# One attention decode step on one core: the first load, wq, issued as two DMAs of 16 and 112 rows instead of one of 128

## The chip, the core and the metric

The kernel runs on one core of a Trainium2 chip. The metric is the device time of one execution in microseconds (us); runs of the kernel before lie between 2516.09 and 2516.40 us, with a median of 2516.12 us. The core has a matrix engine (PE, whose weight loads are listed as PEld), a vector engine (DVE), a scalar engine (ACT), GpSimd (POOL) and a synchronisation engine (SP). In this kernel SP issues nearly all loads from device memory (HBM) into on-chip memory (SBUF, 128 partitions); sixteen DMA engines carry them out. "SPq" in the profile is SP's time spent on issuing.

## What is computed

One query token passes through an attention block with a long cache, and through a small gated feed-forward block. The two results are mixed with a gate made from the same token. There are 32 heads of 128 elements, and each head has 65536 cached keys and values.

```python
g = sigmoid((x * gate_w).sum(-1, keepdims=True))        # x: [1, 1, 512]
q = (x @ wq).reshape(1, 1, 32, 128).transpose(0, 2, 1, 3)   # wq: [512, 4096]
scores = einsum("bhqd,bhkd->bhqk", q, k_cache) * 128 ** -0.5
p = softmax(scores)
o = einsum("bhqk,bhkd->bhqd", p, v_cache)
a = o.transpose(0, 2, 1, 3).reshape(1, 1, 4096) @ wo
b = (silu(x @ w_gate) * (x @ w_up)) @ w_down
out = g * a + (1 - g) * b
```

The two caches have 32 x 65536 x 128 bf16 elements each, 537 MB each; wq is 4.19 MB. The profile counts 1087.64 MB read from HBM in one execution.

## The kernel before

**Streaming.** A head's keys are read in pairs of tiles of 8.39 MB: each of the 128 partitions receives one run of 65,536 bytes. `K_bufs` holds two such pairs and `V_buf` one. For each K tile DVE multiplies the keys by the query (L283) and adds halves of the products (L295, L313); PE adds up what is left (L517), DVE folds it into scores (L324), ACT takes exponentials (L421), and PE multiplies the values by them (L541). There are 64 pairs. The first two and the last two are written out by hand; `prologue` holds the first two, and loops run over the rest.

**Order.** There is no scheduler: each engine runs its instructions in the order in which the code emits them, and `wait` (L171) puts a wait on a semaphore ahead of one. An `Events` object (L28) counts: each DMA adds 16 to its semaphore when it has landed. SP's order decides the order of the loads. A K or V load is issued when its buffer is free, that is, when the instruction that used the buffer last has counted (`load_v` L202, `load_k` L211).

**The start.** `prologue` (L566) begins with two small loads on ACT's queue: the token x into `xT` and the gate weights into `gwT`, 128 rows of 8 bytes each. On SP's queue come, without any wait between them, wq into the first half of `V_buf` (L570), the two tiles of the first K pair (L189), the second K pair (L185), and w_gate and w_up (L576). Row p of the wq load goes into partition p and is one run of 32 KB (four rows of the matrix, 4 x 4096 x 2 bytes). SP then waits until PE has finished with wq (L628) and issues w_down into its place (L629).

**What uses wq.** PE waits for x and for wq (L585, L586) and forms the queries in eight groups of four heads (`query_row`, L590, matmuls at L593). Every matmul reads all 128 partitions of wq, so none can begin before the last row has landed. The query of head 0 is spread over the partitions as `q_sb` (L622). DVE's first product (L283, called at L634) waits for this and for the first K tile.

**What follows in SP's queue.** The third K pair is issued when PE has finished with the first (L669, `pe_D` at 2), the first V pair when the feed-forward block has finished with `V_buf` (L698), and the fourth K pair when PE has finished with the second (L709). From there on the loops run.

Of the kernel before, what the change touches and what calls it, by code (L numbers as in the profile page):

```python
# [10 lines left out]
P = 128  # L11
# [29 lines left out]
def kernel(  # L41
# [18 lines left out]
    _, H, Sk, Dh = A_k_cache.shape  # L60
    D = A_x.shape[2]
    F = B_w_gate.shape[1]
    KT = D // P
# [21 lines left out]
    V_buf = ring.tile([P, PAIR * Dh], bf16, name="V_buf")  # L85
# [51 lines left out]
    def v_view(n):  # L137
        return {N - 4: K_half[0][1], N - 3: V_half[0], N - 2: V_half[1], N - 1: K_half[1][1]}[n]

    sync, act, dve, pool, pe = nc.sync, nc.scalar, nc.vector, nc.gpsimd, nc.tensor  # L140
# [13 lines left out]
    x_in, gw_in, wq_in, ka_in, kb_in, kc_in, wg_in, wu_in, wd_in, vA_in, vB_in = (  # L154
        Events(nc, n, 16)
        for n in ("x_in", "gw_in", "wq_in", "ka_in", "kb_in", "kc_in", "wg_in", "wu_in", "wd_in", "vA_in", "vB_in")
    )
# [13 lines left out]
    def wait(engine, events, value):  # L171
        key = id(engine), id(events)
        value -= taken.get(key, 0)
        if seen.get(key, 0) < value:
            engine.wait_ge(events.sem, value)
            seen[key] = value
# [34 lines left out]
    def load_k(m):  # L211
        if m in (0, M - 1):
            for n in range(2):
                load_tile(K_half[m % 2][n], A_k_cache, 2 * m + n, (k_in[1] if m else ka_in, kb_in)[n])
        else:
            load_pair(K_bufs[m % 2], A_k_cache, m, k_in[m % 2] if m > 1 else kc_in)
# [349 lines left out]
    def prologue():  # L566
        with nc.allow_non_contiguous_dma(reason="small"):
            x_in(act.dma_start(out=xT, in_=A_x[0, 0, :].rearrange("(p t) -> p t", t=KT)))
            gw_in(act.dma_start(out=gwT, in_=gate_w.rearrange("(p t) -> p t", t=KT)))
        wq_in(sync.dma_start(  # L570
            out=V_buf[:, : KT * H * Dh], in_=A_wq.rearrange("(p t) f -> p (t f)", t=KT)
        ))
        load_k(0)
        load_k(1)
        for w, (rows, events) in enumerate(((B_w_gate, wg_in), (B_w_up, wu_in))):
# [7 lines left out]
        dv(dve.memset(rs, 0.0))  # L583

        wait(pe, x_in, 16)  # L585
        wait(pe, wq_in, 16)  # L586

        wait(pe, dv, marks["ones_b"])

# [34 lines left out]
        for c in range(3, H // QUAD):  # L624
# [28 lines left out]
            out=rest[0:1, :], in0=gval[0:1, :], scalar1=-1.0, scalar2=1.0, op0=ALU.mult, op1=ALU.add  # L653
# [40 lines left out]
        for i, a in enumerate(a_ps):  # L694
            pe.matmul(
                a, lhsT=ones_f[0:1, 0:1], rhs=b_sb[:, i * HD : (i + 1) * HD], start=True, stop=False
# [102 lines left out]
    with tc.tile_critical(sync_engine=mybir.EngineType.Pool):  # L799
        prologue()  # L800
        for m in range(2, M):
            if m < M - 1:
                sync_step(m)
            tell_of_v(m - 2)
        sync_end()
        sync_out()
        with act.Fori(0, GROUPED, QUAD) as first:
            scalar_round(first)
        scalar_end()
        with dve.Fori(0, (M - 4) // (2 * MH)):  # L810
            vector_round()
        vector_end()
        with pe.Fori(0, (M - 4) // 2):
            for m in range(2):
                tensor_step(m)
        tensor_end()
        for engine in (pe, act, dve):
            engine.sem_inc(done.sem, 1)

        pool.wait_ge(done.sem, 4)  # L820
        pool.sem_clear(range(first_sem.num, last_sem.num + 1))
        sync.wait_ge(out_in.sem, 16)
        sync.sem_inc(out_in.sem, -16)
# [30 lines left out]
```

## Time and profile before

| what | value |
|---|---|
| median of three runs | 2516.12 us |
| the profiled execution, its own time | 2516.13 us |
| its span, first to last instruction | 2514.3 us |
| DVE busy | 2003.3 us, 80% |
| PE busy | 1489.5 us, 59% |
| ACT busy | 186.9 us, 7% |
| read from HBM | 1087.64 MB |
| mean rate over the span | 433 GB/s |
| wq: issue to landing | 12.4 us, one DMA of 4096 KB |
| x: issue to landing | 12.6 us, 1 KB |
| first K pair, two tiles: issue to landing | 21.9 and 31.2 us, 4096 KB each |
| second K pair: issue to landing | 50.0 us |

"Issue to landing" runs from the start of the issuing instruction to the semaphore count that tells that all data are there. The sixteen DMA engines work through what is queued, so for all but the first load it contains the time spent behind earlier loads. Busy time of an engine is the sum of its instructions' times; an engine that is not the bottleneck may idle without cost. In the page, the span is cut into 40 equal slices of 62.86 us; the line "DMA" gives the busy share of the DMA engines in tenths and "GB/s" the rate in each slice.

### The profile page before, as it was taken

What the parts mean: (1) busy time and instruction counts of PE and PEld (TensorE: products, weight loads), DVE (VectorE), ACT (ScalarE), POOL (GpSimd) and SP (SyncE); (2) the same over time, 40 slices, a digit from 0 to 9 for tenths busy, and PEclk for the clock granted to TensorE, in tenths of its full rate; (3) what the DMA queues carried; (4) which work ended last, traced back from release to release, by engine and by line L of the source; (5) the groups of instructions that cost most, each with busy time, mean ns of one, the idle gap of its engine ahead of it and who ended that gap; (6) DMA issues with size and microseconds to landing.
All of it is one profiled execution on the core that took longest, in us unless ns stands there. A gap on an engine that the chain in (4) does not pass through costs nothing. (4 is left out here: it accounts for less than half of the span.)

```text
span 2514.3 us, 15594 instructions
## 1 busy us (share of the span) xinstructions
PE 1489.5 (59%) x6525; PEld 615.9 (24%) x6525; DVE 2003.3 (80%) x678; ACT 186.9 (7%) x512; POOL 0.7 (0%) x6
## 2 busy tenths in 40 slices
PE   3655746656557456465575564655755646557569
PEld 1322222222222222222222222222212222222223
DVE  6897887877878878779788788787787877977881
ACT  1000000000000000000000000000000000000000
POOL 0000000000000000000000000000000000000000
PEclk8777878778778787787787777877877778778789
DMA  9999999999999999999999999999999999999999
GB/s 413 440 434 433 435 435 435 434 435 434 434 434 434 434 434 434 434 434 436 434 435 436 435 435 434 435 435 434 435 434 434 434 434 435 435 434 434 435 428 394
DMA packets 22606, 1087.80 MB, mean 433 GB/s; under 512 B 2753, under 2 KB 3266, under 8 KB 4546
## 3 DMA queue, kind: packets, MB, share of 16 engines
q1 hardware_dynamic: 22306, 1087.65, 99.9%
q8 instruction: 7, 0.11, 0.0%
q10 hardware_dynamic: 288, 0.00, 0.0%
q14 instruction: 5, 0.04, 0.0%
HBM read 1087.64 MB, written 0.00 MB: 433 GB/s over the span
## 5 line engine op out<-in xcount | busy, mean ns | idle before, releaser
L283 DVE TENSOR_TENSOR K_buf<-K_buf,q_sb 128x16384 bf16<-128x16384 bf16 (+1 forms) x129 | 1112.0, 8620 | 348.2 <-DMA K_buf<-in_A_k_cache_dram 348.2
L517 PE MATMUL S_ps<-K_buf,ident_b 128*128 128x512 bf16 (+1 forms) x1104 | 383.8, 522 | 861.0 <-PEq L513 834.8
L541 PE MATMUL O_ps<-V_buf,P_sb 128*4 128x512 bf16 x3968 | 866.8, 379 | 30.2 <-PEq L513 29.8
L541 PEld LDWEIGHTS O_ps<-V_buf,P_sb 128*4 128x4 bf16 x3968 | 333.0, 85 | 561.8 <-issue 59.3
L295 DVE TENSOR_TENSOR K_buf<-K_buf 128x4096 bf16<-128x4096 bf16 (+1 forms) x127 | 433.7, 3415 | 3.1
L517 PEld LDWEIGHTS S_ps<-K_buf,ident_b 128*128 128x128 bf16 x1104 | 132.9, 125 | 1090.1 <-issue 1030.2
L313 DVE TENSOR_TENSOR K_buf<-K_buf 128x8192 bf16<-128x8192 bf16 x60 | 265.5, 4425 | 2.0
L396 ACT ACTIVATE O_sb<-O_ps 4x512 f32<-4x512 f32 x63 | 63.3, 1005 | 1705.1 <-PE qm_ps L531 1675.1
L324 DVE TENSOR_REDUCE S_sb<-S_ps 128x128 f32<-128x512 f32 x128 | 88.1, 689 | 105.4 <-PE S_ps L517 103.3
L534 PE MATMUL qm_ps<-diag,ones_f 128*128 128x128 f32 x126 | 33.7, 354 | 72.2 <-PEq L513 70.2
L549 PE MATMUL oh_ps<-ident_f,O_sb 4*128 4x1 f32 x504 | 64.3, 244 | 19.6 <-PEq L513 19.6
L549 PEld LDWEIGHTS oh_ps<-ident_f,O_sb 4*128 4x128 f32 x504 | 60.7, 186 | 49.7 <-issue 49.7
L295 DVE TENSOR_TENSOR T_sb<-K_buf 128x2048 bf16<-128x2048 bf16 x60 | 72.8, 1214 | 0.0
L517 PE MATMUL S_ps<-T_sb,ident_b 128*128 128x512 bf16 x240 | 64.7, 391 | 0.0
L534 PEld LDWEIGHTS qm_ps<-diag,ones_f 128*128 128x128 f32 x126 | 21.7, 216 | 76.3 <-issue 76.3
L396 ACT ACTIVATE bias<-top 128x1 f32<-128x1 f32 x32 | 6.5, 203 | 436.7 <-DVE top L334 436.7
L537 PE MATMUL tot_ps<-rs,ones_f 128*128 128x2 f32 (+1 forms) x126 | 24.7, 266 | 17.8 <-PEq L513 17.7
L396 ACT ACTIVATE oT<-whole_o,rg 32x1 f32 (+1 forms) x115 | 33.8, 294 | 4.6
L421 ACT ACTIVATE P_sb<-S_sb,bias 128x256 bf16<-128x256 f32 x62 | 31.5, 508 | 1.0
L537 PEld LDWEIGHTS tot_ps<-rs,ones_f 128*128 128x128 f32 x126 | 20.2, 202 | 36.8 <-issue 36.8
L517 PEld LDWEIGHTS S_ps<-T_sb,ident_b 128*128 128x128 bf16 x240 | 20.7, 96 | 15.9
L330 DVE TENSOR_REDUCE m<-S_sb 128x1 f32<-128x512 f32 x32 | 22.0, 686 | 1.1
(68 smaller groups left out, 209.8 us busy)
## 6 DMA issues: line engine op xcount, KB each, us to landing
K_buf<-in_A_k_cache_dram SPq DMA_DIRECT2D x4, 4096.0 KB, 32.5
V_buf<-in_A_v_cache_dram SPq DMA_DIRECT2D x2, 4096.0 KB, 21.4
V_buf<-in_A_v_cache_dram SPq DMA_DIRECT2D x4, 2048.0 KB, 18.2
V_buf<-in_A_wq_dram SPq DMA_DIRECT2D x1, 4096.0 KB, 12.4
K_buf<-in_A_v_cache_dram SPq DMA_DIRECT2D x1, 4096.0 KB, 30.2
K_buf<-in_A_wo_dram SPq DMA_DIRECT2D x7, 512.0 KB, 16.2
K_buf<-in_A_v_cache_dram SPq DMA_DIRECT2D x3, 1024.0 KB, 23.2
V_buf<-in_B_w_gate_dram SPq DMA_DIRECT2D x1, 1792.0 KB, 54.5
```

Source lines behind the costliest of these rows:

```text
L283: return own[0](dve.tensor_tensor(out=K, in0=K, in1=q_rep, op=ALU.mult))
L295: ins = dve.tensor_tensor(out=to, in0=K[:, :, 0:half], in1=K[:, :, half : 2 * half], op=ALU.add)
L313: dve.tensor_tensor(out=K[:, :, 0:half], in0=K[:, :, 0:half], in1=K[:, :, half:], op=ALU.add).then_inc(c_S[0], 1)
L324: return own[0](dve.tensor_reduce(out=S_sb[h % 2][:, g * NB : (g + 1) * NB], in_=S_ps[n % 2], axis=AXIS.X, op=ALU.add))
L330: (dv_max if h else dv_first)(dve.tensor_reduce(out=m_sb[:, 0:1], in_=S_sb[h % 2], axis=AXIS.X, op=ALU.max))
L396: return act.activation(out=out, in_=in_, func=ACT.Copy, scale=scale)
L421: return act.activation(out=out, in_=S_sb[h % 2][:, b * PAIR : b * PAIR + count], func=ACT.Exp, bias=bias[:, 0:1], scale=scale, accum_out= ...
L517: ins = pe.matmul(S_ps[n % 2][:, start:stop, :], lhsT=ident_b, rhs=src[:, start:stop, c : c + QUAD], start=(c == 0), stop=(c == width - QUAD),
L534: pe.matmul(mT, lhsT=ones_f, rhs=diag, start=True, stop=True).then_inc(pe_m.sem, n)
L537: pe_t(pe.matmul(tot[:, :n], lhsT=ones_f, rhs=rs[:, :n], start=True, stop=True))
L541: ins = pe.matmul(O_ps, lhsT=probs[:, j : j + 4], rhs=view[:, j : j + 4, :], start=(opens and j == start), stop=(closes and j == stop - 4),)
L549: ins = pe.matmul(oh, lhsT=O_sb[:, c * Dh : (c + 1) * Dh], rhs=ident_f[0:4, c : c + 1], start=(opens and c == 0), stop=(c == 3),)
```

## The change

The load of wq is issued as two DMAs on the same queue, the first with rows 0 to 15, the second with rows 16 to 127. Source, destination, bytes and the length of a row are the same. The wait of PE asks for a count of 32 instead of 16, as two DMAs now add 16 each.

```diff
-        wq_in(sync.dma_start(
-            out=V_buf[:, : KT * H * Dh], in_=A_wq.rearrange("(p t) f -> p (t f)", t=KT)
-        ))
+
+        for a, b in ((0, 16), (16, P)):
+            wq_in(sync.dma_start(
+                out=V_buf[a:b, : KT * H * Dh], in_=A_wq.rearrange("(p t) f -> p (t f)", t=KT)[a:b]
+            ))
         load_k(0)
         load_k(1)
...
         wait(pe, x_in, 16)
-        wait(pe, wq_in, 16)
+        wait(pe, wq_in, 32)
```

On SP the instruction list becomes one DMA longer: a copy of 16 x 16384 elements and one of 112 x 16384 stand where one of 128 x 16384 stood. The other engines keep their lists.

## The prediction

> **What bounds the kernel now.** I began with the page's slices, to see whether the load stream ever pauses.
>
> ```profile
> span 2514.3 us, 15594 instructions
> ...
> DMA  9999999999999999999999999999999999999999
> GB/s 413 440 434 433 435 435 435 434 435 434 434 434 434 434 434 434 434 434 436 434 435 436 435 435 434 435 435 434 435 434 434 434 434 435 435 434 434 435 428 394
> ```
>
> Between the third slice and the 38th the rate stays at 433 to 436 GB/s, although DVE and PE work unevenly. Only the first slice and the last two fall below. The stream sets the time: 1087.65 MB at 434.5 GB/s take 2503 us of the 2514.3, and the rest is start and end. DVE, busy 80%, follows the loads:
>
> ```profile
> DVE K_buf L283 <- DMA K_buf<-in_A_k_cache_dram: 348.2, 64, 21.9
> ```
>
> That is from the list of waits (total us, times, longest): DVE waits for 64 loads of keys, 348.2 us in all. So DMA time lost anywhere is paid at the end, and DMA time gained early is earned. Next the timeline of the start (start us, duration, engine, line):
>
> ```profile
> 0.89 0.40 SPq L570 DMA_DIRECT2D V_buf<-in_A_wq_dram  x1
> 0.90 0.41 ACTq L568 DMA_DIRECT2D xT<-in_A_x_dram  x1
> ...
> 1.35 0.89 SPq L189 DMA_DIRECT2D K_buf<-in_A_k_cache_dram  x2
> ...
> 2.28 0.61 SPq L185 DMA_DIRECT2D K_buf<-in_A_k_cache_dram  x1
> ...
> 13.52 3.47 PE L593 MATMUL S_ps<-V_buf,xT 128*1 128x512 bf16 x8 [13.52 <-DMA xT<-in_A_x_dram]
> ...
> 18.66 0.25 ACT L396 ACTIVATE q_sb<-qm_ps 128x128 bf16<-128x128 f32 x1
> ...
> 23.26 8.69 DVE L283 TENSOR_TENSOR K_buf<-K_buf,q_sb 128x16384 bf16<-128x16384 bf16 x1 [21.90 <-DMA K_buf<-in_A_k_cache_dram]
> ```
>
> SP issues its first loads with no gap. x, only 1 KB, lands as late as wq, so PE starts at 13.52. The first query is ready at 18.91, yet DVE starts at 23.26, when the first K tile lands: the query has 4.35 us to spare, the load stream nothing. Last, the DMA rates of the first 4 us, in slices of 0.1 us (packets counted where they start):
>
> ```profile
> GB/s 0 0 0 0 0 0 0 0 0 0 0 0 0 0 0 0 0 0 0 2294 983 655 0 328 0 655 328 0 0 0 0 0 0 0 0 0 0 328 983 1311
> ```
>
> The first row starts at 1.9 us, 1.0 after the issue of wq. Sixteen rows (each 32 KB adds 328 to a slice) start up to 2.7 us, one on each DMA engine; the next ones start from 3.7.
>
> **The unit.** At 434.5 GB/s the sixteen engines carry 27.2 GB/s each, so a row of 32 KB takes 1.21 us. The 128 rows are eight to an engine, 9.7 us; wq's 12.4 us from issue to landing are 1.0 before the first row, these 9.7, and 1.7 of slow start and completion.
>
> **The change, part by part.** (1) *One more issue on SP.* The rows beside it take 0.40 (wq), 0.45 (half of 0.89) and 0.61 us. All issues behind the first move back by 0.4 to 0.6 us, the last, w_up, from 3.53 to about 4.0. The cover is wq itself: its rows keep the engines busy until about 12.4 us, and the K tile behind it needs only to be queued by then. Without that cover it would cost those 0.4 to 0.6. Should a full queue hold SP back longer, w_up is what waits; its data are used at 61.8 us, and SP's next own work is at 25.02. Cost 0.
>
> (2) *The wait for 32.* No instruction is added on PE, and what stands behind this wait (all queries, then the first product) is released by x anyway, which lands with the last wq rows. Cost 0; a count that comes up to 4.35 us later than now, relative to the K tile, is still hidden.
>
> (3) *The start.* With one row for each engine the first DMA could be set up faster. The issue takes 0.40 us now and the engines' first rows start over some 0.7 us, so at most 1.1 us are to be had; at worst nothing. I take 0.2: most of the 1.0 us between issue and first data is neither of the two.
>
> (4) *Where the rows go.* Every load in this trace that matters fills all 128 partitions, each engine serving its own eight. The flat 434.5 GB/s shows sixteen paths of 27.2, but not whether a path belongs to the engine that reads or to the eight partitions that are written. If to the engine: one row, then seven, eight as before, 0 us. If to the partitions, and to eight neighbours: the 16 rows go through two paths, eight in series, 9.7 us in place of 1.21, a loss of 8.5 us during which fourteen paths idle. The other 112 rows then have 14 paths with eight rows each, 9.7 against 8.5, and 1.2 more are lost if nothing overlaps. So 0 to +9.7, with no row nearer to one end than to the other: no load here writes a part of the partitions. I take the end at the partitions without the last 1.2, +8.5. I choose it because a DMA of 16 rows is the first thing here that sends all sixteen engines into one eighth of the memory, and nothing in the trace frees that from sharing.
>
> [...] No run before this one shows a load on fewer partitions.
>
> *Sum.* 2514.3 + 0 + 0 - 0.2 + 8.5 = 2522.6 us of span; the profiled execution had 1.8 outside it (2516.13), so 2524.4. Its time and the median (2516.12) are the same. Nothing gives the 8.5 back: the K tiles, the third K pair (issued at 55.90, on PE's word) and every later load move along. With SP's V loads landing 24.4 us after issue and needing 19.3 for 8.39 MB, about 5 us of work stays queued ahead of each, so an engine that is late by 8.5 sets the pace, and others that are less late only use up that reserve.
>
> **The rivals.**
>
> *A. Not slower: the path belongs to the engine.* Then only (3) is left: 2516.1 - 0.2 = 2515.9, at the very best 2515.0. [...] Against it: only loads over all partitions have been seen. It decides from the point where the 16 rows land within about 4 us of their issue (1.0 + 1.21 + the 1.7).
>
> *B. A small loss.* Four engines to a path in the 16 rows, four row-times in place of one, 3 x 1.21 = 3.6 us, and the 112 rows dealt out evenly: 2516.1 + 3.6 - 0.2 = 2519.5, say 2519 to 2521. For it: 16 rows are few. Against it: 112 rows in sevens do not fit groups of eight.
>
> *C. A large loss.* The 112 rows are dealt to the engines in turn, so that sixteen neighbours are always written at once. With four to a path, 32 row-times in place of 8: 24 x 1.21 = 29 us, 2545; with eight, 56 x 1.21 = 68 us, 2584. For it: the trace does not show which rows an engine takes. Against it: in the 128-row loads the same dealing would have shown as a rate far below 434.5.
>
> *D. The code does not do what it says.* Both DMAs stand on SP in the order written, so I give this nothing of its own.
>
> **How the numbers follow.** The forecast, sharing in the 16 rows and in the sevens, has 0.46 (its own range 2520.5 to 2529); A 0.25; B 0.13; C 0.08; 0.08 is left for what I have not thought of, 0.03 of it faster by more than A, 0.05 slower. The range from 2515.0 to 2529 takes in A, B and nearly all of the forecast, and leaves out C and most of the rest. For this kernel a change of less than 0.2%, 5.0 us, counts as none: the bounds are 2511.1 and 2521.2. Slower is nearly all of the forecast (0.44), C, 0.05 of the rest and a bit of B: 0.59. The same is A, most of B and the low end of the forecast: 0.38. Faster, beyond anything that (3) can give: 0.03.
>
> **What would show it.** The 16-row DMA's landing: 7 (four to a path: 1.0 + 4.85 + 1.7) to 12 us after its issue if the partitions set the rate, about 4 if the engines do. The 112-row DMA's landing: near 21 us after the first issue in place of 12.4. PE's first matmul near 22 us, DVE's first product near 31.8, the third K pair's issue near 64. The first slice falls from 413 GB/s by up to 8.5 x 434.5 / 62.86 = 59, less if only some engines are late by that much; the slices behind it keep 434. Wrong would be a first slice at 413 with the same start of DVE's product at 23.3 (A), or a loss that appears in later slices, for which I have no mechanism.

## The result and the profile after

The changed kernel takes 2525.74 us (median of 7 runs, 2524.84 to 2526.16), the kernel before 2516.14 (7 runs, 2516.08 to 2516.89): 9.6 us more, a ratio of 1.0037 with a 95% interval of 1.0025 to 1.0048. The profiled execution took 2526.16 us, with a span of 2524.3.

The page of the changed kernel, its span, its DMA share and its rate in 40 slices:

```profile
span 2524.3 us, 15595 instructions
...
DMA  9999999999999999999999999999999999999999
GB/s 354 444 426 435 433 435 434 432 433 435 433 435 435 436 433 433 432 434 434 437 435 435 432 433 433 433 436 436 436 433 433 432 433 434 438 434 435 433 430 387
```

The first slice falls from 413 to 354 GB/s. Over its 62.86 us these 59 GB/s are 3.7 MB, the work of 8.5 us at 434.5 GB/s. Behind it little is added: in the next stretch of 62.86 us the rate is 434 in place of 440 GB/s, another 0.9 us, and from there to 2388.6 us it is 434 in both. So the loss is made at the start and kept. The busy share, nine tenths and more everywhere, does not show it: an engine that carries a row slowly counts as busy (a share of 1.02 at 243 GB/s, below).

The timeline of the start, and the answers on the two wq loads (KB each, us from issue to landing):

```profile
0.89 0.85 SPq L572 DMA_DIRECT2D V_buf<-in_A_wq_dram  x2
...
1.79 0.90 SPq L189 DMA_DIRECT2D K_buf<-in_A_k_cache_dram  x2
...
22.90 3.57 PE L595 MATMUL S_ps<-V_buf,xT 128*1 128x512 bf16 x8 [22.90 <-DMA V_buf<-in_A_wq_dram]
```

```profile
V_buf<-in_A_wq_dram SPq DMA_DIRECT2D x1, 3584.0 KB, 21.5
...
V_buf<-in_A_wq_dram SPq DMA_DIRECT2D x1, 512.0 KB, 6.5
```

```profile
32.48 8.69 DVE L283 TENSOR_TENSOR K_buf<-K_buf,q_sb 128x16384 bf16<-128x16384 bf16 x1 [31.12 <-DMA K_buf<-in_A_k_cache_dram]
```

The issue of the second DMA costs SP 0.45 us. The 112 rows land about 22.8 us into the span (13.3 before), PE starts at 22.90 (13.52), now released by wq and no longer by x, and DVE begins at 32.48 (23.26), still released by the K tile. DVE is 9.2 us late. Near the end PE is 9.3 us late, in the kernel before and then in the changed one:

```profile
2384.54 13.97 PE O_ps L541 x64
```

```profile
2393.84 13.97 PE O_ps L541 x64
```

The span grows by 10.0: the other 0.7 of this execution arise at the end, where the last load of wo lands at 2519.82 in place of 2509.81.

The rate while the 112 rows are written, and below it that of the kernel before at full stream (from and to in us, length, busy time of PE, PEld, DVE, ACT and POOL, PE's clock, DMA share, GB/s; a packet counts where it starts):

```profile
5.30:20.40 15.10, 0.00 (x0) 0.00 (x0) 0.00 (x0) 0.00 (x0) 0.00 (x0) 1.00 1.02 243
```

```profile
13.50:23.20 9.70, 9.65 (x54) 3.24 (x55) 0.00 (x0) 4.36 (x10) 0.00 (x0) 1.00 1.01 433
```

How long one row takes can be read from the DMA queue's own lines: packets that started in a stretch, their MB, and their time as a share of what sixteen engines have in it. The kernel before from 1 to 3 us comes first, then the changed kernel from 1 to 3 and from 7 to 20.2 us:

```profile
q1 hardware_dynamic: 16, 0.52, 94.2%
```

```profile
q1 hardware_dynamic: 16, 0.52, 180.2%
...
q1 hardware_dynamic: 96, 3.15, 92.7%
```

The first sixteen rows took 1.88 us each before (94.2% of 2 us) and 3.60 in the changed kernel, and 96 of the 112 rows took 2.04, where a row at full stream takes 1.21. At 243 GB/s the 3.67 MB of the 112 rows take 15.1 us, not 8.4: most of the loss lies in the larger DMA.

### The profile page after: what moved, and what is told of

The parts are those of the page before. It is cut to its first block, busy times and chain, and to the rows that moved or that the text cites. A ratio compares the mean times of both kernels' runs of the same rounds, so it can differ in the third digit from the quotient of the medians.

```text
span 2524.3 us, 15595 instructions
## 1 busy us (share of the span) xinstructions
PE 1489.2 (59%) x6525; PEld 615.5 (24%) x6525; DVE 2003.4 (79%) x678; ACT 186.9 (7%) x512; POOL 0.7 (0%) x6
## 5 line engine op out<-in xcount | busy, mean ns | idle before, releaser
L534 PEld LDWEIGHTS qm_ps<-diag,ones_f 128*128 128x128 f32 x126 | 21.9, 218 | 76.5 <-issue 76.5
L595 PE MATMUL S_ps<-V_buf,xT 128*1 128x512 bf16 x32 | 10.6, 470 | 22.9 <-DMA V_buf<-in_A_wq_dram 22.9
## 6 DMA issues: line engine op xcount, KB each, us to landing
V_buf<-in_A_wq_dram SPq DMA_DIRECT2D x1, 3584.0 KB, 21.5
```

What stands on the lines that cost most here:

```text
L534: pe.matmul(mT, lhsT=ones_f, rhs=diag, start=True, stop=True).then_inc(pe_m.sem, n)
```

## The experiments

Each is the kernel before with another way of loading wq. The code is shortened: `wq_rows` stands for wq with one row per partition, `W` for a row's 16384 elements, and PE waits for 16 counts per DMA of wq. Times are medians, and 2516.2 us stands for the kernel before in its runs beside them (2516.16 to 2516.28).

### Is it the second DMA, or the partitions it leaves out?

**e1** cuts wq by columns, so that both DMAs fill all partitions.

```diff
+for a, b in ((0, 2048), (2048, W)):
+    wq_in(sync.dma_start(out=V_buf[:, a:b], in_=wq_rows[:, a:b]))
...
+wait(pe, wq_in, 32)
```

> wq as two DMAs cut by columns: 128 rows of 4 KB, then 128 rows of 28 KB. The bytes of the first DMA are those of the 16-row DMA, the partitions all 128. If the partitions written set the rate: no loss, 2516 us within 1 us, wq landing about 12.4 us after its first issue. If a second DMA or a small first one costs by itself: about +9.6 as in the changed kernel, 2525 us. If the order in which rows are read from HBM matters: no loss either, as engines read from all over the matrix.

Measured: 2516.16 us, ratio 1.0000 (0.9990 to 1.0009). Its two loads:

```profile
V_buf<-in_A_wq_dram SPq DMA_DIRECT2D x1, 3584.0 KB, 12.2
...
V_buf<-in_A_wq_dram SPq DMA_DIRECT2D x1, 512.0 KB, 3.7
```

The same bytes in the same two portions land in 3.7 and 12.2 us in place of 6.5 and 21.5. A second DMA, a small DMA in front, one more issue and a wait for 32 cost nothing that can be measured.

**e2** cuts wq into two halves of 64 rows.

```diff
+for a, b in ((0, 64), (64, P)):
+    wq_in(sync.dma_start(out=V_buf[a:b, :W], in_=wq_rows[a:b]))
```

> wq as two DMAs of 64 rows each, partitions 0-63 and 64-127. If the partitions written set the rate, two engines share a path for all of wq: at full sharing 8 row-times of 2.43 us instead of 1.21, +9.7, 2526 us; at the 1.75 to 2.25 us per row that the 112-row DMA showed, +4 to +8, 2520 to 2524 us. If only the 16-row DMA is at fault: 2516 us. If each extra DMA costs: about 2525 us.

Measured: 2526.76 us, ratio 1.0042 (1.0025 to 1.0059). No DMA of 16 rows is left, and the loss is 10.5 us: it is not special to a small DMA. Of the two ends the expectation gave, full sharing by two (+9.7) is the nearer.

**e3** cuts wq into eight DMAs of 16 rows (`range(0, P, 16)` in the same loop).

> wq as eight DMAs of 16 neighbouring rows. If the partitions written set the rate: every row-time is like that of the first 16 rows in the changed kernel (3.4 to 3.9 us with the start in it), so about 8 x 3.6 = 29 us instead of 9.7, +19, 2535 us; at full sharing by four, 8 x 4.85 = 39, +29, 2545 us; by eight, +68, 2584 us. If only the number of small DMAs matters and each costs its issue (0.4 us) behind running data: 2516 us; if the cost is per extra DMA as in the changed kernel, 7 x 9.6 = +67, 2583 us.

Measured: 2541.68 us, ratio 1.0101 (1.0084 to 1.0118): +25.4, between the +19 read off the first row-time of the changed kernel and the +29 of full sharing by four, far from 0, +67 and +68.

**e4** writes as e3 does, but reads every eighth row.

```diff
+for i in range(8):
+    wq_in(sync.dma_start(out=V_buf[16 * i : 16 * (i + 1), :W], in_=wq_rows[i:P:8]))
```

> Eight DMAs into 16 neighbouring partitions each, as in e3, but each reads every eighth row of wq, so the sources are spread as widely as they can be; wq is thereby permuted and the queries are wrong, the work is the same. If the partitions written set the rate: as e3 within 1 us. If neighbouring sources in HBM are the cause: 2516 to 2518 us.

Measured: 2541.72 us, e3's time within 0.04 us. Where the rows come from in HBM makes no difference that can be measured. Where they go does: e5 below reads the same rows as e4, writes them elsewhere and takes 2526.15 us.

### Which partitions share a path?

**e5** writes and reads every eighth row.

```diff
+for i in range(8):
+    wq_in(sync.dma_start(out=V_buf[i:P:8, :W], in_=wq_rows[i:P:8]))
```

> Eight DMAs of 16 rows as in e3, but each takes every eighth row and writes every eighth partition, so the output is right. If a path belongs to eight neighbouring partitions: one engine to a path, no loss, 2516 to 2517 us. [...] If it is the number of small DMAs that cost in e3: 2541.7 us again.

Measured: 2526.15 us, ratio 1.0032 (1.0014 to 1.0049): neither of the two times expected, but near e2's 2526.76.

**e6** cuts wq into four DMAs of 32 neighbouring rows (`range(0, P, 32)`).

> wq as four DMAs of 32 neighbouring rows, two rows to each engine. If a path belongs to eight neighbouring partitions: four engines to a path, as in e3, about 2541 us. [...]

Measured: 2525.85 us, ratio 1.0031 (1.0013 to 1.0049): not the 2541 expected, and again near e2.

The rates while wq is written, in stretches of the same columns as above: e3 first, then e5, e6 and e2.

```profile
7.80:34.80 27.00, 0.00 (x0) 0.00 (x0) 0.00 (x0) 0.00 (x0) 0.00 (x0) 1.00 1.02 117
```

```profile
7.80:20.60 12.80, 0.00 (x0) 0.00 (x0) 0.00 (x0) 0.00 (x0) 0.00 (x0) 1.00 0.99 205
```

```profile
7.80:20.60 12.80, 0.00 (x0) 0.00 (x0) 0.00 (x0) 0.00 (x0) 0.00 (x0) 1.00 0.99 205
```

```profile
7.80:20.60 12.80, 0.00 (x0) 0.00 (x0) 0.00 (x0) 0.00 (x0) 0.00 (x0) 1.00 1.01 207
```

All four stretches show a full DMA share (0.99 to 1.02), so it is not that fewer engines carry rows; each row takes longer. The kernel before has 433 GB/s (13.5 to 23.2 us). Sixteen neighbouring partitions take 117 GB/s, a quarter of it and a little more; 16 partitions in steps of eight, or 32 neighbours, 205, a little less than half; 64 neighbours (e2) 207. That a DMA into 32 partitions and one into 64 get the same rate (205 and 207 GB/s), and that a step of eight gets it too, refutes paths of eight neighbouring partitions, by which e5 would have lost nothing and e6 25 us. The runs do not show which partitions lie together beyond these cases.

### What does each part of the change cost alone?

**e7** puts one more DMA of rows 0 to 15 ahead of the 128-row load; **e8** does the same with rows 16 to 127 (`(a, b) = (16, 128)`).

```diff
+more_in(sync.dma_start(out=K_bufs[1][a:b, : KT * H * Dh], in_=wq_rows[a:b]))
 wq_in(sync.dma_start(out=V_buf[:, : KT * H * Dh], in_=wq_rows))
 load_k(0)
+wait(sync, more_in, 16)
 load_k(1)
```

> The load of 128 rows of before, and ahead of it one more DMA that loads rows 0 to 15 of wq into a buffer not yet in use (the second K pair is issued after it has landed). It shows what the 16-row DMA costs alone. Its bytes cost 1.2 us on any theory. If sixteen engines share four paths as in e3 (4.5 us per row): 2516.2 + 4.5 = 2520.7 us, or about 2519 if the slow start covers part of it; if this DMA carries all of the loss of the changed kernel: 2516.2 + 9.6 + 1.2 = 2527 us; if it costs its bytes only: 2517.4 us.

> As e7, with rows 16 to 127 in the additional DMA. Its bytes cost 8.5 us on any theory. If the 112 rows collide too: the loss of the changed kernel without the part of the 16 rows, 9.6 less 2 to 3.3, so 2516.2 + 8.5 + 6.3 to 7.6 = 2531 to 2532.3 us; if they do not: 2524.7 us.

Measured: e7 2519.60 us (2519.48 to 2519.72; ratio 1.0006, 0.9988 to 1.0023), e8 2530.23 us (2529.72 to 2531.49; ratio 1.0048, 1.0030 to 1.0066). The interval of e7 includes 1, so by it alone e7 cannot be told from no change; that its small cost is real rests on its ten runs, which lie within 0.24 us, and on e10 below, whose interval is clear of 1. Less their bytes (1.2 and 8.5 us) the 16 rows cost 2.1 to 2.2 us and the 112 rows 5.5. Neither part carries all of the loss, and 2 of the 9.6 us are missing. e8 came out below the 2531 to 2532.3 expected of a collision.

**e9** and **e10** put these DMAs behind the 128-row load, at full stream.

> As e8, with the additional DMA of rows 16 to 127 behind the 128-row load instead of ahead of it, so that its rows run at full stream and not in the slow start. In e7 and e8 the two parts cost 2.1 and 5.5 us beyond their bytes, together 7.5 of 9.6. If the slow start hides part of a collision: more than in e8, 2516.2 + 8.5 + 7.5 = about 2532 us. If the missing 2 us come from the 112 rows following right behind the 16: 2530.2 us as in e8.

> As e7, with the additional DMA of 16 rows behind the 128-row load. If the slow start hid part of its cost in e7 (2519.6 us): 4.5 us for the row-time of e3, 2520.7 us. If it did not: 2519.6 us again.

Measured: e9 2530.92 us (ratio 1.0057, 1.0040 to 1.0073), e10 2520.95 us (1.0018, 1.0008 to 1.0027). The 16 rows cost 3.5 us there beyond their bytes, 1.3 more than at the start; the expected 2520.7 holds. The slow start does hide part of a collision: a first row takes 1.88 us there even in the kernel before and not 1.21, which is 0.7 of the 1.3. For the 112 rows e9 lies between both expectations, 6.2 us beyond the bytes.

**e11** loads rows 0 to 111 first, then rows 112 to 127.

> wq as rows 0 to 111, then rows 112 to 127. Both parts collide as in the changed kernel, in the other order. If each part costs what it costs at that place: 112 rows at the start 5.5 (e8), 16 rows at full stream 3.3, together 8.8, 2525 us. If it is the order, a small DMA ahead of a large one, that costs: 2516 to 2518 us.

Measured: 2524.95 us, ratio 1.0033 (1.0021 to 1.0046), as adding the parts had it. The order is not the cause.

**e12** has both additional DMAs, with the 128-row load between them.

> Both additional DMAs of e7 and e9 in one kernel: rows 0 to 15, then the 128-row load, then rows 16 to 127. Their bytes cost 9.7 us. If the two parts only add up (2.1 of e7 and 6.2 of e9): 2516.2 + 9.7 + 8.3 = 2534.2 us, and the 1.3 us by which the changed kernel loses more come from the 112 rows standing right behind the 16. If the parts cost 9.6 whenever both are there: 2535.5 us.

Measured: 2534.83 us (4 runs, 2534.37 to 2535.72), 0.6 and 0.7 us from the two numbers: inconclusive. The parts of e7 and e9 explain 8.3 of the 9.6 us and leave 1.3. DVE's first product is a second measure, which leaves out what happens later in the run (one execution each; e7, e9, e12):

```profile
26.92 8.69 DVE L283 TENSOR_TENSOR K_buf<-K_buf,q_sb 128x16384 bf16<-128x16384 bf16 x1 [25.56 <-DMA K_buf<-in_A_k_cache_dram]
```

```profile
37.85 8.69 DVE L283 TENSOR_TENSOR K_buf<-K_buf,q_sb 128x16384 bf16<-128x16384 bf16 x1 [36.49 <-DMA K_buf<-in_A_k_cache_dram]
```

```profile
42.03 8.69 DVE L283 TENSOR_TENSOR K_buf<-K_buf,q_sb 128x16384 bf16<-128x16384 bf16 x1 [40.67 <-DMA K_buf<-in_A_k_cache_dram]
```

Against 23.26 in the kernel before, and less their bytes, they are late by 2.5, 6.1 and 9.1 us, the changed kernel by 9.2. By this measure the parts add up to 8.6, and only 0.6 us are open at the start; e12, with the parts apart, loses as much as the changed kernel. That the 112 rows suffer from standing right behind the 16 is therefore not shown. Which seven rows an engine takes was not tried either.

No experiment points to a version that beats the kernel before: e1 is the harmless way to make the first load smaller, and it gains nothing.

## Why the prediction was right

**What bounds the kernel** held. The 9.2 us by which DVE starts late are in the end time, and nothing later gave them back or added much (the median grew by 9.6).

**(1) One more issue** and **(2) the wait for 32**: forecast at 0, and e1, which has both, measures 0.

**(3) The start**: forecast at -0.2. The rates of the first 4 us of the changed kernel show the sixteen first rows starting between 1.9 and 2.3 us, up to 2.7 before:

```profile
GB/s 0 0 0 0 0 0 0 0 0 0 0 0 0 0 0 0 0 0 0 2621 983 1311 328 0 0 0 0 0 0 0 0 0 0 0 0 0 0 0 0 0
```

So the part of the gain that comes from the faster start of the engines is real, at most 0.4 us, and drowns: the next rows, which began at 3.7 us before, have not begun at 4. e1 did not turn a small first DMA into time either.

**(4) Where the rows go**: the choice of the partitions' side was right (e3 and e4, 2541.68 and 2541.72 us, against e1, 2516.16), and rival A, which put the path on the engine's side, falls with it. The size of the sum was near, 8.5 forecast against 9.6, but its two terms were not. I had given the 16 rows all of it, eight in series on paths of eight neighbours, and taken nothing for the 112. Measured, the 16 rows cost 2.1 at the start (e7), where about four and not eight engines share a path, an estimate from e3's 117 of 433 GB/s, and part of that hides in the slow start, and the 112 rows 5.5 to 6.2 alone (e8, e9), some 7.5 in place if the 16 cost 2.1 there too (9.6 less 2.1). Two errors of opposite sign met, so that the sum came out near is luck; what was right is that the partitions written set the rate (e4 and e5 read the same rows, at 117 and 205 GB/s).

**The rivals.** B had the 112 rows dealt out evenly, without loss; e8 and e9 show a loss of 5.5 and 6.2. C, sixteen neighbours at a time for all of wq, is what e3 builds: 25.4 us, near C's 29 with four to a path. Its premise does not hold for the 112-row DMA, which ran at 243 GB/s and not at 117. Four engines to a path, in B, C and the landing time of the 16 rows, was a supposition that no row of the kernel before shows; for sixteen neighbours e3's 117 of 433 GB/s bears it out. Row length is the same before and after the change; rows of 28 KB (e1, 427 GB/s from 4 to 10 us) and of 64 KB (the K pairs, 434) ran at rates within 2% of each other.

**What would show it.** Near 21 us for the 112 rows' landing, counted from the first issue: 21.9. PE near 22: 22.90. DVE near 31.8: 32.48. The first slice down by up to 59 GB/s: 59. The third K pair's issue near 64: 64.65. Only the 16 rows landed a little earlier than said, 6.5 us after issue against 7 to 12. The terms given for four to a path make 7.55 and not 7, and the row took 3.60 us in place of 4.85.

## What to carry to other kernels

A load that fills a subset of the partitions can run at a half or a quarter of the rate (205 and 117 of 433 GB/s here), even with all engines at work and a full DMA share (0.99 and 1.02), and in this kernel, which is bound by its load stream, all of that was paid: 9.2 us at DVE's first product, 9.6 at the end. To make a first load smaller, cut it along the row (e1, free) and not across the partitions (e2, e3, e5, e6: 10 to 25 us for 4 MB). When a sum comes out right, measure its terms all the same: here two wrong ones nearly cancelled.

## What the runs showed of the hardware

- At full stream one of the sixteen engines carries 27.2 GB/s (434.5 / 16). e3's 16 neighbours together take 117 GB/s, 4.3 times that, and the partitions of e5 and e6 205 GB/s, 7.5 times that. If these are four paths and eight, an estimate from the rates, four engines on one path move 29 GB/s and two move 26. A 32 KB row takes 4.5 and 2.6 us there, against 1.21.
- The number of partitions alone is not what counts: 16 of them in steps of eight (e5) are as fast as 64 neighbours (e2): 205 and 207 GB/s.
- The times scatter by 1.3 us in the changed kernel (2524.84 to 2526.16), by 0.4 in e5 (10 runs, 2525.97 to 2526.34), and by 2.0 in e2 (4 runs, 2526.10 to 2528.14), whose two DMAs have 64 rows each. The cause stays open.
